# One list of 3388 program steps, put in another order

## Chip, core and metric

One core of a Trainium2 chip runs the whole kernel in one launch. The metric is the device time in microseconds (us); lower is better. Five instruction streams run side by side and meet at semaphores: TensorE (PE, with its weight loads PEld), VectorE (DVE), ScalarE (ACT), GpSimd (POOL) and the sync engine (SP), which issues nearly all DMAs.

## The reference, cut

```python
def reference(**kwargs):
    attn_out = _attn_ref(**attn_kwargs)   # 4 batches x 8 heads, 512 local + 32 global queries, head size 64
    x = attn_out.transpose(0, 2, 1, 3).reshape(B * S, H * D)          # 2176 x 512
    x = _moe_ref(x=x, **moe_kwargs)       # max(x@w1, x@w2, x@w3) @ w_out, width 768
    return _moe2_ref(x=x, **moe2_kwargs)  # (sigmoid(x@w_gate) * (x@w_val)) @ w_out2, width 1536
```

The local queries see a window of 32 positions to each side and the 32 global keys; the global queries see everything. All of it is float32.

## The kernel before

The kernel computes in stages that overlap. Attention is cut into 32 units t = 0 to 31 (4 batches x 2 halves of the sequence x 4 pairs of heads). Four units make a chunk c = 0 to 7 of 256 or 288 tokens, and each chunk then goes through the first feed-forward layer (the maximum of three products, and its output product). After the last chunk come the gate and value products over all tokens (line L1048) and the output product (L1235); these two use seven products in place of eight for a 2x2 block product. Float32 precision is kept by splitting an operand in a high and a low part and adding three products (`mm3`, L321 to L323).

Every piece of work is a generator whose parts are put into a list `ev`: 3388 steps, each a few instructions, with a planned time (L1303 onwards). The order in which the steps are run, and so the order of each engine's instruction stream, isn't the planned one, though: it is the list `ORDER` (L22) of 3388 step numbers, written out. Each engine works through its own steps strictly in that order. If a step waits, all later steps of that engine wait with it.

The steps that are named below; the last number of a step is its part:

- lg(c, what): whole-chunk loads of q, k, v for the first two chunks (`at_load_group`, L422). lqk(t): 8 loads of q and k of a unit (L517, L518). lv(t): 4 loads of v into the tile vr (`load_v_rows`, L497 to L503), of which there is one buffer only. g(b, 0): loads of the global queries and values (L384, L389); g(b, 1): their transpose on DVE (L392).
- pqk(t, .): transposes of q and k. sc(t, 0): the score products (L627). sm(t, .): softmax on ACT and DVE, whose part 11 is the last subtraction into pc on DVE (L715) and whose part 12 is a transposing DMA pt<-pc on SP (L718). smg is the same for the global queries, with the DMA in part 7 (L761).
- pv(t, .): v is split in three 16-bit parts: part 0 casts on ACT (L599), 1 subtracts on POOL (L601), 2 casts on DVE (L603), 3 subtracts on POOL (L605) and is the last to read vr. lv(t) must therefore wait for pv(t-1, 3), and pv(t, 0) for the landing of lv(t).
- av(t, 0), avg(t, .), scg(t, 0): the products with v, and those of the global queries. l1(c, f, w, 0): 12 products of the first layer (L892, L906 and L900 read the result); l2(c, m, .): 18 products of its output. wa(i, 0): load of a weight block (L302, L305).

`at_load_group`, `load_v_rows` and the other generators are not touched by the change.

Of the kernel before, what the change touches and what calls it, by code (L numbers as in the profile page):

```python
# [22 lines left out]
    57, 153, 186, 154, 155, 304, 56, 59, 187, 120, 0, 62, 58, 63, 64, 67, 68, 69, 74, 75, 70, 121, 161, 71, 162, 76,  # L23
    77, 78, 1861, 1862, 79, 5, 6, 163, 1863, 1864, 156, 188, 7, 8, 122, 1854, 1855, 95, 96, 166, 167, 168, 1856, 80,
    1865, 1857, 97, 1833, 123, 81, 82, 1858, 1866, 1826, 194, 100, 101, 189, 102, 103, 195, 98, 87, 88, 72, 9, 10, 11,
    104, 12, 1827, 1828, 337, 13, 173, 14, 83, 128, 15, 129, 99, 107, 289, 108, 105, 109, 60, 110, 1834, 169, 208, 170,
    130, 131, 111, 112, 1829, 209, 231, 1835, 106, 174, 89, 133, 1830, 124, 157, 232, 233, 113, 16, 90, 114, 91, 115,
    1831, 116, 190, 175, 176, 134, 135, 136, 137, 198, 1840, 199, 125, 200, 140, 141, 142, 143, 177, 1836, 178, 117,
    144, 145, 126, 305, 92, 93, 1847, 1841, 223, 279, 179, 61, 1875, 180, 224, 225, 226, 1903, 84, 203, 181, 1848, 182,
    1849, 204, 205, 146, 206, 147, 148, 207, 280, 85, 86, 236, 234, 149, 150, 256, 1850, 257, 1851, 1842, 210, 211,  # L30
    1837, 1843, 1844, 241, 237, 242, 264, 212, 213, 171, 138, 191, 214, 215, 192, 158, 1867, 1868, 201, 238, 159, 1322,
    1324, 281, 1852, 1904, 1876, 1859, 290, 227, 239, 265, 1323, 1877, 216, 1905, 1869, 1917, 1326, 17, 243, 1860,
    1870, 1325, 1878, 1879, 1906, 244, 240, 1832, 312, 132, 245, 246, 313, 314, 284, 1882, 1889, 1890, 164, 217, 1896,
    1327, 139, 1880, 218, 1316, 1314, 285, 286, 247, 248, 1891, 1871, 1872, 1315, 1907, 287, 288, 1892, 196, 1893,
    1853, 249, 1938, 315, 1883, 1884, 1885, 165, 250, 1897, 1898, 1899, 266, 1900, 1901, 317, 1902, 1317, 1910, 1886,
    1338, 1339, 318, 360, 362, 1340, 1341, 73, 1939, 183, 319, 1342, 202, 251, 1940, 338, 1845, 118, 1911, 219, 252,
    1931, 320, 321, 1918, 151, 267, 1343, 1952, 1846, 1919, 1932, 1933, 228, 229, 1941, 363, 324, 291, 1912, 1881, 253,
    292, 1934, 293, 325, 1330, 1332, 1942, 1, 396, 1344, 326, 1318, 294, 1331, 316, 268, 258, 1920, 160, 230, 1935,
    364, 1319, 368, 1328, 259, 260, 261, 1924, 282, 283, 1838, 1921, 235, 1980, 269, 197, 295, 1953, 270, 296, 1945,
    398, 271, 262, 263, 1334, 1908, 1913, 399, 1914, 2, 297, 1839, 1954, 1887, 1894, 1333, 298, 1925, 1348, 1926, 339,  # L40
    94, 369, 1981, 1335, 306, 1909, 299, 300, 1955, 1956, 1946, 1947, 1959, 1346, 370, 1354, 371, 152, 327, 328, 329,
    372, 1948, 1355, 1336, 1949, 18, 19, 1895, 404, 220, 1329, 1960, 322, 1961, 1927, 1928, 1888, 323, 273, 1962, 274,
    1982, 275, 1347, 1349, 1963, 330, 1356, 1357, 20, 331, 307, 308, 21, 272, 22, 400, 23, 332, 1358, 1973, 333, 1350,
    1966, 24, 25, 345, 1974, 1975, 309, 1976, 1929, 1977, 1967, 1983, 26, 340, 341, 342, 373, 1984, 1968, 1969, 184,
    185, 254, 334, 1970, 375, 1930, 1987, 376, 405, 1985, 127, 1988, 1337, 221, 310, 406, 343, 1351, 1989, 27, 1366,
    28, 1359, 1374, 407, 1957, 1990, 1991, 365, 1367, 1375, 411, 468, 335, 361, 470, 377, 378, 412, 471, 379, 346, 413,
    408, 432, 347, 1958, 3, 4, 380, 1362, 366, 434, 388, 1986, 472, 1376, 1363, 1370, 276, 1371, 344, 414, 348, 349,
    415, 381, 416, 350, 435, 436, 401, 193, 1368, 1369, 437, 382, 438, 1873, 445, 383, 367, 351, 1377, 352, 440, 389,
    390, 1992, 311, 1874, 1964, 354, 353, 409, 391, 1965, 355, 356, 357, 384, 1364, 397, 417, 1372, 385, 1993, 1922,
    1923, 336, 473, 591, 1378, 358, 424, 1320, 1386, 425, 386, 418, 441, 504, 301, 419, 420, 1387, 1388, 1389, 277,  # L50
    1379, 426, 1978, 255, 1979, 1915, 476, 1390, 1380, 1382, 442, 427, 1391, 359, 278, 29, 447, 428, 448, 1936, 1937,
    1373, 443, 444, 593, 1381, 449, 450, 1383, 387, 1402, 506, 507, 421, 1384, 1916, 451, 1392, 1396, 422, 1971, 477,
    483, 433, 478, 484, 1394, 1393, 512, 479, 640, 480, 1403, 460, 594, 474, 1385, 452, 446, 392, 1352, 393, 1972, 423,
    1395, 1397, 1950, 453, 508, 454, 455, 456, 457, 458, 481, 461, 462, 485, 1406, 1398, 1399, 1404, 1943, 1418, 540,
    1400, 1405, 1407, 595, 1353, 513, 596, 514, 542, 459, 1410, 486, 1360, 515, 482, 516, 519, 410, 429, 520, 463, 464,
    465, 521, 522, 487, 488, 489, 466, 543, 544, 641, 490, 509, 510, 523, 1944, 1401, 469, 599, 1419, 172, 491, 524,
    492, 525, 493, 494, 1951, 1422, 1408, 1409, 496, 497, 600, 627, 601, 1365, 498, 1411, 30, 606, 1412, 499, 607,
    1413, 1414, 1415, 430, 222, 602, 431, 603, 1416, 1417, 1420, 1421, 608, 500, 609, 394, 610, 1423, 611, 526, 467,
    597, 1424, 527, 528, 374, 495, 1361, 612, 613, 614, 505, 1425, 1321, 1438, 545, 1426, 529, 1427, 530, 615, 531,
    546, 547, 1428, 1439, 532, 548, 1440, 549, 517, 553, 550, 551, 555, 533, 678, 534, 535, 616, 395, 501, 502, 552,  # L60
    302, 1430, 503, 1466, 402, 629, 556, 557, 558, 559, 560, 561, 630, 631, 562, 1431, 1442, 563, 564, 565, 1441, 536,
    635, 1443, 541, 604, 617, 1432, 537, 566, 567, 636, 637, 554, 638, 639, 1468, 576, 577, 1467, 1469, 578, 579, 568,
    569, 570, 571, 572, 642, 643, 1470, 1429, 1471, 1444, 1445, 605, 1434, 680, 65, 580, 581, 714, 582, 592, 1446,
    1450, 1447, 1435, 1472, 1436, 663, 1448, 1454, 1452, 644, 403, 645, 573, 681, 583, 585, 664, 646, 586, 1449, 1451,
    1453, 786, 686, 647, 1455, 619, 475, 648, 620, 621, 622, 687, 1458, 688, 716, 1456, 649, 650, 1457, 31, 32, 1473,
    689, 651, 1462, 690, 652, 1460, 1459, 717, 33, 34, 538, 628, 1461, 1433, 587, 574, 575, 1463, 655, 1464, 653, 656,
    632, 693, 1474, 727, 35, 1475, 36, 1478, 1437, 1476, 588, 589, 37, 38, 39, 1477, 1479, 1486, 1482, 1465, 1484, 40,
    657, 41, 722, 42, 750, 584, 691, 694, 1483, 1485, 1487, 654, 1480, 658, 598, 1481, 1490, 679, 695, 1502, 665, 723,
    729, 666, 724, 730, 752, 1488, 667, 668, 1489, 1491, 725, 590, 731, 1503, 696, 1504, 618, 511, 669, 670, 697, 1498,
    698, 623, 753, 754, 1492, 1493, 726, 1499, 732, 733, 624, 788, 789, 699, 718, 700, 701, 706, 707, 659, 660, 661,  # L70
    734, 822, 1500, 1501, 858, 662, 692, 682, 702, 703, 704, 625, 708, 709, 672, 673, 674, 675, 676, 539, 1494, 677,
    735, 736, 737, 1495, 758, 626, 738, 739, 794, 795, 796, 740, 1506, 824, 715, 922, 825, 683, 1507, 759, 633, 1530,
    760, 761, 1531, 742, 743, 1508, 1510, 1509, 1496, 1511, 909, 1538, 1512, 765, 766, 767, 1513, 744, 762, 797, 768,
    826, 769, 1532, 1533, 719, 1534, 770, 798, 1497, 745, 1535, 1536, 710, 634, 1516, 741, 771, 772, 773, 774, 775,
    1514, 119, 705, 1537, 711, 763, 776, 66, 860, 751, 778, 830, 831, 777, 1515, 832, 1539, 1518, 779, 801, 833, 802,
    780, 1542, 1517, 1519, 803, 1540, 781, 782, 684, 804, 805, 837, 806, 861, 827, 807, 834, 808, 1526, 809, 866, 783,
    871, 671, 835, 810, 811, 712, 713, 799, 1520, 1521, 787, 814, 815, 812, 1541, 1543, 43, 1522, 911, 836, 816, 746,
    894, 895, 813, 1524, 1544, 1523, 1525, 1527, 1545, 1528, 912, 913, 1546, 867, 1547, 873, 868, 1345, 874, 869, 875,
    1548, 1549, 817, 1505, 818, 823, 850, 1550, 1529, 755, 1551, 945, 996, 1552, 1553, 851, 1554, 784, 785, 870, 876,
# [1407 lines left out]
```

## Time and profile before

| what | us |
|---|---|
| median of 3 runs (lowest, highest) | 803.16 (800.95, 805.37) |
| the profiled execution's own time | 803.19 |
| its span, first to last instruction | 801.5 |
| TensorE busy in the span | 785.0 (98%) |
| TensorE weight loads busy | 753.7 (94%) |
| VectorE, ScalarE, GpSimd busy | 567.8, 471.6, 141.7 |

The profile is read by asking, for TensorE, in which stretches it is idle and what ended each idle time, and then by following what the releasing engine had itself waited for. A line of a timeline gives start, length, engine, line and tiles; a square bracket at its end tells how long the engine was idle just before and who ended that. "SPq" is the sync engine issuing DMAs.

### The profile page before, as it was taken

What the parts mean: (1) busy time and instruction counts of PE and PEld (TensorE: products, weight loads), DVE (VectorE), ACT (ScalarE), POOL (GpSimd) and SP (SyncE); (2) the same over time, 40 slices, a digit from 0 to 9 for tenths busy, and PEclk for the clock granted to TensorE, in tenths of its full rate; (3) what the DMA queues carried; (4) which work ended last, traced back from release to release, by engine and by line L of the source; (5) the groups of instructions that cost most, each with busy time, mean ns of one, the idle gap of its engine ahead of it and who ended that gap; (6) DMA issues with size and microseconds to landing.
All of it is one profiled execution on the core that took longest, in us unless ns stands there. A gap on an engine that the chain in (4) does not pass through costs nothing.

```text
span 801.5 us, 18202 instructions
## 1 busy us (share of the span) xinstructions
PE 785.0 (98%) x6950; PEld 753.7 (94%) x6950; DVE 567.8 (71%) x1249; ACT 471.6 (59%) x1131; POOL 141.7 (18%) x149
## 2 busy tenths in 40 slices
PE   6999999999999999999999999999999999999998
PEld 5888899989899989899999999999999999999998
DVE  4768788667766676774586866777565669977673
ACT  6998867455565564463467665665645466443441
POOL 3125574242323423132110000000000000000000
PEclk9999999999999999999999999999999999999999
DMA  8978464545536564345145464857142578542521
GB/s 238 294 183 222 86 123 87 107 97 103 115 73 122 101 112 89 67 99 159 38 153 186 115 226 159 289 167 242 69 143 105 162 240 312 189 142 86 172 66 53
DMA packets 208887, 116.08 MB, mean 145 GB/s; under 512 B 152864, under 2 KB 191264, under 8 KB 208800
## 3 DMA queue, kind: packets, MB, share of 16 engines
q1 hardware_dynamic: 208512, 114.80, 52.6%
q8 instruction: 54, 0.88, 0.5%
q14 instruction: 33, 0.27, 0.1%
q10 hardware_dynamic: 288, 0.13, 0.1%
HBM read 74.91 MB, written 28.57 MB: 129 GB/s over the span
## 4 chain that ended last, share of the span: by engine, by line
PE 80%; SPq 7%; ACT 5%; DMA 3%; DVE 2%; issue 1%; POOL 1%; ACTq 0%; DVEq 0%; POOLq 0%
PE pa L1048 18%; PE pe L1048 9%; PE pa L1235 9%; PE ps L321 7%; PE ps L323 6%; PE ps L322 6%; PE pb L1048 4%; PE pe L1235 4%; PE ps L892 4%; PE sp L627 3%; PE pb L1235 2%; DMA vr<-in_v_g_dram 2%; SPq L518 2%; SPq L517 1%; PE ps L928 1%
## 5 line engine op out<-in xcount | busy, mean ns | idle before, releaser
L1048 PE MATMUL pa<-m,m 128*128 128x384 f32 (+1 forms) x864 | 154.4, 326 | 0.0
L321 PE MATMUL ps<-xt,m 128*128 128x288 f32 (+1 forms) x504 | 148.1, 294 | 3.9 <-DVE h L906 2.3
L323 PE MATMUL ps<-xt,m 128*128 128x288 f32 (+1 forms) x504 | 146.4, 290 | 0.0
L322 PE MATMUL ps<-xt,m 128*128 128x288 f32 (+1 forms) x504 | 145.3, 288 | 0.8 <-DVE stg L732 0.8
L1048 PEld LDWEIGHTS pa<-m,m 128*128 128x128 f32 x864 | 144.1, 188 | 0.1
L321 PEld LDWEIGHTS ps<-xt,m 128*128 128x128 f32 x504 | 94.7, 188 | 8.6 <-DVE h L906 3.0
L322 PEld LDWEIGHTS ps<-xt,m 128*128 128x128 f32 x504 | 94.7, 188 | 1.0 <-DVE stg L732 1.0
L323 PEld LDWEIGHTS ps<-xt,m 128*128 128x128 f32 x504 | 94.8, 188 | 0.0
L1054 ACT COPY sn<-pa 128x384 f32<-128x384 f32 (+1 forms) x108 | 49.3, 461 | 74.1 <-PE pa L1048 71.3
L1048 PE MATMUL pe<-m,m 128*128 128x384 f32 (+1 forms) x432 | 81.7, 327 | 0.2 <-DVE sgt L1067 0.2
L1048 PEld LDWEIGHTS pe<-m,m 128*128 128x128 f32 x432 | 72.6, 188 | 0.6 <-DVE sgt L1067 0.6
L1235 PE MATMUL pa<-m,m 128*128 128x256 f32 x576 | 72.2, 283 | 0.0
L1235 PEld LDWEIGHTS pa<-m,m 128*128 128x128 f32 x576 | 70.5, 192 | 0.1
L669 ACT ACTIVATE sm<-sm,st 128x224 f32<-128x224 f32 x128 | 60.8, 480 | 16.0 <-DVE st L633 15.6
L906 DVE TENSOR_TENSOR h<-ps,h 128x288 f32<-128x288 f32 (+1 forms) x90 | 39.1, 436 | 32.0 <-PE ps L323 22.3
L715 DVE TENSOR_TENSOR pc<-sm,pc 64x512 f16<-64x512 f32 (+1 forms) x72 | 51.5, 718 | 4.4 <-ACT pc L712 3.4
L271 POOL TENSOR_TENSOR h<-h,h 128x288 fp32r<-128x288 f32 (+1 forms) x42 | 36.0, 862 | 91.8 <-ACT h L911 90.6
L633 DVE CUSTOM_DVE_ANT_0 sm<-sp,mask 128x224 f32<-128x224 f32 x128 | 44.8, 382 | 8.7 <-PE sp L627 6.9
L1178 DVE TENSOR_TENSOR m<-m,m 128x768 fp32r<-128x768 f32 x44 | 40.7, 954 | 13.5 <-ACT m L1173 13.0
L321 PE MATMUL ps<-h,m 128*128 128x288 f32 (+1 forms) x168 | 49.2, 293 | 0.0
L322 PE MATMUL ps<-h,m 128*128 128x288 f32 (+1 forms) x168 | 48.6, 289 | 0.6 <-POOL h L271 0.5
L323 PE MATMUL ps<-h,m 128*128 128x288 f32 (+1 forms) x168 | 48.9, 291 | 0.0
(193 smaller groups left out, 1573.7 us busy)
## 6 DMA issues: line engine op xcount, KB each, us to landing
m<-in_moe_w_dram SPq DMA_DIRECT2D x18, 512.0 KB, 5.8
gd<-sgt SPq DMA_DIRECT2D x48, 192.0 KB, 2.7
m<-gd SPq DMA_DIRECT2D x6, 1536.0 KB, 7.2
m<-in_moe_w_val_dram SPq DMA_DIRECT2D x6, 1024.0 KB, 5.6
wr<-in_moe_w_out_dram SPq DMA_DIRECT2D x6, 1024.0 KB, 6.0
m<-in_moe_w_gate_dram SPq DMA_DIRECT2D x5, 1024.0 KB, 5.6
vr<-in_v_l_dram SPq DMA_DIRECT2D x48, 96.0 KB, 2.5
x2d<-x2s SPq DMA_DIRECT2D x32, 128.0 KB, 2.0
```

The costliest lines, as they stand in the source:

```text
L271: nc.gpsimd.tensor_tensor(out=out, in0=a, in1=f32(b), op=ALU.subtract)
L321: nc.tensor.matmul(ps, lhsT=wh, rhs=xh, start=first, stop=False)
L322: nc.tensor.matmul(ps, lhsT=wh, rhs=xl, start=False, stop=False)
L323: nc.tensor.matmul(ps, lhsT=wl, rhs=xh, start=False, stop=last)
L633: nc.vector.tensor_tensor_reduce(out=sm[:, hh, j], in0=sp[hh][:, j, 0:224], in1=mask[:, half + j, :], scale=-SC, scalar=3.0e38, op0=ALU.ad ...
L669: nc.scalar.activation(sm4[:, i], sm4[:, i], AF.Exp, bias=st[:, 0, i:i + 1], scale=-1.0, accum_out=st[:, 2, i:i + 1])
L715: nc.vector.tensor_tensor(out=l_, in0=s_, in1=h_, op=ALU.subtract)
L906: nc.vector.tensor_tensor(out=a, in0=ps[:, 0:n], in1=a, op=ALU.max)
L1048: nc.tensor.matmul(ps, lhsT=w[l][:, a, i], rhs=x[m][:, i], start=(k in (1, 2, 5) and i + l + m == 0), stop=(k in (2, 3, 4) and i == 1 and ...
L1054: nc.scalar.copy(t[:, 0:n], pend[u]["a"][:, 0:n])
L1178: tt(out=lo, in0=src[op], in1=f32(hi), op=ALU.subtract)
L1235: nc.tensor.matmul(ps, lhsT=g[l][:, f], rhs=wo_op(b, f, m), start=(k in (1, 2, 5) and f + l + m == 0), stop=(k in (2, 3, 4) and f == 5 and ...
```

## The change

`ORDER` is replaced by another permutation of the same 3388 numbers. Nothing else differs: the same steps, instructions, tiles and transfers. According to its author the new list is the outcome of a search on a model of the schedule in which the sync engine is held longer by each transfer. 423 of the 650 TensorE steps stand at another place among TensorE's steps, most of them by a few places; each unit and chunk is begun within a few us of TensorE work of where it was.

The diff is 346 lines of numbers. Of it, the lines with the steps that are spoken of:

```diff
 ORDER = [
-    57, 153, 186, 154, 155, 304, 56, 59, 187, 120, 0, 62, 58, 63, 64, 67, 68, 69, 74, 75, 70, 121, 161, 71, 162, 76,
...
-    1865, 1857, 97, 1833, 123, 81, 82, 1858, 1866, 1826, 194, 100, 101, 189, 102, 103, 195, 98, 87, 88, 72, 9, 10, 11,
...
-    1453, 786, 686, 647, 1455, 619, 475, 648, 620, 621, 622, 687, 1458, 688, 716, 1456, 649, 650, 1457, 31, 32, 1473,
...
-    729, 666, 724, 730, 752, 1488, 667, 668, 1489, 1491, 725, 590, 731, 1503, 696, 1504, 618, 511, 669, 670, 697, 1498,
...
-    1514, 119, 705, 1537, 711, 763, 776, 66, 860, 751, 778, 830, 831, 777, 1515, 832, 1539, 1518, 779, 801, 833, 802,
...
-    1048, 793, 908, 1632, 1624, 1037, 943, 991, 944, 1123, 1027, 1028, 1049, 1050, 1045, 1140, 992, 1081, 993, 994,
...
-    1033, 995, 1060, 1658, 1051, 1176, 1052, 1142, 1660, 55, 1053, 1082, 1054, 1659, 1055, 1124, 1056, 1057, 1058,
...
+    87, 88, 89, 0, 57, 56, 58, 62, 59, 186, 187, 63, 64, 67, 90, 91, 68, 69, 70, 256, 74, 75, 76, 71, 77, 161, 162,
...
+    1830, 209, 195, 190, 1857, 1858, 72, 105, 106, 128, 129, 130, 337, 1831, 1832, 194, 231, 99, 1833, 1834, 1835, 120,
...
+    585, 631, 786, 1472, 1451, 1453, 1455, 1456, 586, 402, 686, 687, 1473, 31, 621, 622, 632, 1458, 1460, 1459, 693,
+    475, 716, 32, 33, 34, 1462, 652, 653, 1461, 1463, 717, 1457, 35, 628, 36, 37, 1474, 1437, 38, 1464, 1475, 1465,
...
+    725, 668, 1502, 1503, 1504, 695, 1490, 1491, 669, 750, 727, 752, 726, 679, 706, 1492, 696, 403, 1361, 729, 670,
...
+    1026, 989, 943, 944, 1027, 1630, 1631, 1028, 1629, 1040, 1632, 980, 1140, 1022, 1621, 1076, 865, 1041, 1121, 990,
...
+    1079, 1178, 1634, 1635, 1046, 1650, 1660, 1659, 1661, 1060, 1061, 1062, 1662, 1663, 1664, 1063, 1636, 1064, 1637,
...
 ]
```

Numbers and steps: 57, 59, 58 = lg(0, q0), lg(0, q1), lg(0, k1); 195, 194 = lg(1, q), lg(1, k); 1833 = wa(1, 0); 31, 32 = g(2, 0), g(2, 1); 704, 705, 711 = sm(16, 11), sm(16, 12), av(16, 0); 669, 670, 672 = smg(15, 6), smg(15, 7), avg(15, 0); 1027, 1033, 1060 = pv(24, 3), lv(25), pv(25, 0).

The stretch from pv(24, 3) to pv(25, 0), with TensorE's and SP's steps alone:

```text
before: pv(24,3)  scg(25,0)  lqk(28)  scg(26,0)  lv(25)  pv(25,0)
after:  pv(24,3)  l2(4,3,0)  l2(4,3,1)  l2(4,2,3)  sc(25,0)  lqk(28)  l2(4,0,3)  sc(26,0)  avg(23,0)  avg(23,1)
        scg(25,0)  lv(25)  lqk(29)  sm(25,12)  scg(26,0)  sm(24,12)  l1(5,3,0,0)  l1(5,0,0,0)  l1(5,2,0,0)
        l1(5,3,1,0)  pv(25,0)
```

The stretch from g(2, 0) to g(2, 1), with TensorE's steps alone:

```text
before: g(2,0)  g(2,1)
after:  g(2,0)  l1(2,2,0,0)  l1(2,2,1,0)  g(2,1)
```

Loads at the beginning, on SP's list: before lg(0,q0), lg(0,q1), lg(0,k1), wa(5,0), g(0,0), wa(4,0), wa(1,0), wa(0,0), lg(1,k), lg(1,q); after lg(0,q0), lg(0,k1), lg(0,q1), wa(5,0), wa(4,0), g(0,0), wa(0,0), lg(1,q), lg(1,k), wa(1,0).

## Rows read from the trace of the kernel before

**Rows 1.** The page: busy time of each engine; the chain that ended last

```profile
PE 785.0 (98%) x6950; PEld 753.7 (94%) x6950; DVE 567.8 (71%) x1249; ACT 471.6 (59%) x1131; POOL 141.7 (18%) x149
...
PE 80%; SPq 7%; ACT 5%; DMA 3%; DVE 2%; issue 1%; POOL 1%; ACTq 0%; DVEq 0%; POOLq 0%
```

**Rows 2.** Busy time by stretches of 20 us: stretch, engines with instruction counts, clock, DMA

```profile
0.00:20.00 20.00, 13.11 (x118) 10.09 (x120) 9.02 (x36) 13.13 (x42) 7.69 (x27) 1.00 0.87 238
...
160.00:180.00 20.00, 18.57 (x174) 17.44 (x168) 12.74 (x41) 11.31 (x34) 9.91 (x11) 1.00 0.48 96
...
200.00:220.00 20.00, 18.88 (x219) 17.34 (x218) 15.97 (x46) 10.61 (x33) 7.73 (x9) 1.00 0.57 113
...
380.00:400.00 20.00, 20.00 (x152) 19.83 (x152) 11.86 (x16) 8.86 (x16) 3.92 (x3) 1.00 0.14 50
...
500.00:520.00 20.00, 20.00 (x124) 20.00 (x122) 14.78 (x32) 13.48 (x23) 0.00 (x0) 1.00 0.84 280
```

**Rows 3.** Waits of TensorE, whole span: us in total, times, longest

```profile
PE tq L541 <- POOL mask L354: 3.2, 1, 3.2
PE ps L321 <- DVE h L906: 2.3, 3, 1.4
PE sp L627 <- ACT kw L565: 2.3, 3, 0.9
PE tq L541 <- DMA m<-in_q_l_dram: 1.4, 1, 1.4
PE ps L321 <- ACT h L900: 1.2, 2, 0.7
PE ps L322 <- DVE stg L732: 0.8, 1, 0.8
PE ot L788 <- DMA pt<-pc: 0.7, 1, 0.7
PE ps L322 <- POOL h L271: 0.5, 1, 0.5
```

**Rows 4.** Waits of ACT and of DVE for loads, 20 to 400 us

```profile
ACT vb L599 <- DMA vr<-in_v_g_dram: 18.3, 10, 3.1
...
DVE qgt L392 <- DMA qgr<-in_q_g_dram: 4.8, 2, 2.9
```

**Rows 5.** SP's issues of two lines: duration ns min/median/max, first and last start

```profile
L518 SPq DMA_DIRECT2D kr<-in_k_l_dram x96: 311/449/2011, 43.2 to 320.8; - x96
...
L718 SPq DMA_TRANSPOSE pt<-pc x24: 1273/1438/2452, 105.0 to 360.3; - x24
```

**Rows 6.** DMA issues of the page's kind: KB each, median us to landing

```profile
vr<-in_v_g_dram SPq DMA_DIRECT2D x24, 16.0 KB, 2.0
pt<-pc SPq DMA_TRANSPOSE x24, 3.8
```

**Rows 7.** Timeline around the longest wait of TensorE past the start

```profile
162.26 1.88 SPq L384 DMA_DIRECT2D qgr<-in_q_g_dram  x4
...
165.44 0.32 DVE L392 STREAM_TRANSPOSE qgt<-qgr 128x128 f32<-128x128 f32 x1 [2.93 <-DMA qgr<-in_q_g_dram]
...
168.72 0.38 PE L321 MATMUL ps<-xt,m 128*128 128x256 f32 x1 [1.43 <-DVE h L906]
```

**Rows 8.** Timeline from pv(24, 3) to pv(25, 0)

```profile
283.09 1.28 POOL L605 TENSOR_TENSOR vb<-vr,vb 128x512 bf16<-128x512 f32 x1 [1.42 <-DVE vb L603]
...
290.73 0.62 ACT L599 CAST vb<-vr 128x512 bf16<-128x512 f32 x1 [3.06 <-DMA vr<-in_v_g_dram]
...
293.27 0.40 PE L321 MATMUL ps<-xt,m 128*128 128x288 f32 x1 [0.70 <-ACT h L900]
```

**Rows 9.** Timeline of the first 20 us: lg(1, q) and pqk(5, 0)

```profile
13.22 2.57 SPq L431 DMA_DIRECT2D m<-in_q_l_dram  x2
...
19.46 0.66 PE L541 MATMUL tq<-ident,m 128*64 128x128 f32 x8 [1.45 <-DMA m<-in_q_l_dram]
```

**Rows 10.** Waits of SP, whole span

```profile
SPq L718 <- PE ps L323: 10.8, 12, 1.6
```

324 rows, old and new, of the table ORDER are left out of this document.

## Prediction

> **What bounds the kernel now.** I read the busy times first, then the stretches, then TensorE's waits, then the waits of the engines that released it. TensorE is busy 785.0 of 801.5 us and 80% of the chain that ended last is TensorE's [rows 1], so nothing but TensorE's idle time, 801.5 - 785.0 = 16.5 us, can be won by an order that leaves every instruction as it is. The stretches say where it lies [rows 2]: 6.9 us in the first 20, then one or two us in single stretches of the attention part (1.4 in 160 to 180, 1.1 in 200 to 220), and none in 500 to 520, which stands for the whole second half. So the change is decided in the first 360 us. 3.2 us of it is the wait for the first instruction, and about as much comes after the last product; neither list changes that. Some 10 us are left.
>
> TensorE's waits name them [rows 3]: 2.3 us for DVE's h (1.4 of it one wait), 1.4 for a load of q, 1.2 for ACT's h, 0.7 for a transposed pt, 0.5 for POOL's h, 0.8 for stg, and 2.3 for kw at the start. Behind most of them stands SP. The wait of 1.4: DVE stood 2.93 us for qgr, whose four loads SP began to issue at 162.26, and the step that TensorE needed came only after that [rows 7]. The ACT waits: ACT stands 18.3 us in 10 of 24 units before the cast of vr, DVE 4.8 us before qgt [rows 4], and what is queued behind (the copies of h, the softmax) is late; after one of 3.06 us TensorE waited 0.70 [rows 8].
>
> SP is the reason, since it is nearly full. A load holds it 0.449 us, a transposing DMA 1.438 [rows 5]. A unit has 8 + 4 loads and one transpose: 12 x 0.449 + 1.438 = 6.8 us, and the 24 units follow each other every (360.3 - 105.0) / 23 = 11.1 us [rows 5], so units alone take 61% of SP, and the weight loads and stores come on top.
>
> At this point a rule speaks against the change. The Trainium skill (DMA: Bandwidth & Descriptors, "Issuing engines are not separate DMA queues") says that the sequencer's time to start a DMA is usually small beside the DMA itself; then where a load stands on SP's list would hardly matter and the time would stay at 803.2. The trace doesn't bear it out for these loads: 0.449 us of issue against 2.0 to landing, and 61% of SP.
>
> **The change, part by part.** It adds and removes no instruction. I compared the two lists by the TensorE work that stands between a step and the one that needs it; TensorE work is close to time here, since TensorE is 98% busy. A product of 288 columns is 0.132 us (20 us / 152 [rows 2]), so an l1 step of 12 is 1.6 us and an l2 step of 18 is 2.4. The rest is sized likewise from its matmuls' count and pitch: sc 0.9, scg 0.6, avg 0.4 and 0.6.
>
> *The single buffer vr.* From the last read of vr, pv(t-1, 3), to its next use, pv(t, 0), POOL's 1.28 [rows 8], four issues (4 x 0.449) and a landing of 2.0 [rows 6] must fit: 5.1 us. Before, the list gives pv(25, 0) two scg steps, 1.2 us; the true distance was 290.73 - 283.09 = 7.6 us, as lqk(28)'s eight issues stood in between [rows 8]. The new list gives 2.2 (l2 in 256 columns) + 1.8 + 1.0 + 1.2 + 6.4 = 12.6 us. The same count for t = 9 to 31, in us:
>
> before: 2.4 5.7 3.4 8.0 9.8 13.9 4.3 7.4 8.3 4.1 4.4 0.0 13.7 6.6 4.3 11.3 1.2 5.9 4.1 2.2 3.7 4.2 11.5
> after: 3.2 7.3 5.9 7.2 11.6 8.2 7.2 6.7 9.0 9.8 1.6 3.2 5.3 7.0 3.9 8.1 12.6 8.0 6.4 10.3 12.4 3.7 1.4
>
> Under 5.1 are 12 before and 6 after; what is missing sums to 23 us before and 14 after. ACT's waits should fall by the same 40%, from 18.3 to about 11 [rows 4]. TensorE's share of them is at most 1.2 + (2.3 - 1.4) + 0.5 = 2.6 us [rows 3]; 40% is 1.1 us won. Bounds: 2.6, if the six that are left hit where TensorE has other work; 0, if they hit harder (t = 19 and 31 are shorter than before).
>
> *g(2) and g(3).* The load and its use stood together; now two l1 steps, 2.9 us, stand between, and for g(3) as much. DVE's waits were 2.93 [rows 7] and 4.8 - 2.93 = 1.9 [rows 4]. The 1.4 us of TensorE go [rows 7]; bounds 0 to 1.6.
>
> *The transpose for av(16).* sm(16, 12) stood right before av(16, 0); now 22.6 us of TensorE work stand between. The 0.7 us [rows 3] go.
>
> *The first 20 us.* pqk(5, 0) waited 1.45 us for lg(1, q) [rows 9]. The new list issues it ahead of lg(1, k) and wa(1, 0), five issues earlier, so it should land in time: 1.4 won, bounds 0 to 1.4. Against it, lg(0, q1) now goes behind the two issues of lg(0, k1): 2 x 0.449 = 0.9 us later for pqk(3, 0), which may wait 0 to 0.9; TensorE then waits for kw anyway (2.3 in three waits [rows 3]), so I take 0.4.
>
> *What is new and tight.* sc(9), sc(15) and sc(28) stand right behind the DVE transposes that they need, with no TensorE step between. Before, only sc(10) and the first units stand so; sc(10) is in no row of the waits, the first units cost up to 0.9 each [rows 3]. Three times 0 to 0.9; nearest is sc(10), so 0.3 each, 0.9 in all. The second half of the list has the same kind of sequence as before (each product 0.9 us or more behind the copy that frees its bank, the end in the same order), and TensorE is never idle there [rows 2]: nothing, and if DVE's cover there (14.8 of 20 us) failed at a place, some tenths.
>
> Sum: -1.1 - 1.4 - 0.7 - 1.4 + 0.4 + 0.9 = -3.3 us. Against the profiled execution's 803.19, which lies on the median of the runs, 803.16, this gives 799.9 us.
>
> **Rivals.** *All of the order's stalls go.* If the new list leaves none of the 2.6, nor stg's 0.8, and sc costs nothing: -2.6 - 1.4 - 0.7 - 1.4 - 0.8 = -6.9, 796.3 us. For: the waits share one cause. Against: six vr distances are still too short.
>
> *The gain is given back.* Six short distances of vr, of which 19, 20 and 31 are 2 to 4 us short, hit TensorE as hard as those of before, and each sc that stands close costs 0.9: -1.4 - 0.7 - 1.4 + 0.9 + 2.7 = +0.1, so 803.3, no change. The rule on SP's issue time above ends here too.
>
> *Slower: transposes stuck behind loads on SP.* Where a transpose is listed after loads that it doesn't need, av waits for them. From DVE's last step to the product the new list gives smg(15) 3.9 us with 12 loads ahead, sm(10) 4.8 with 8, sm(29) 4.5 with 5, sm(18) 7.5 with 12. Needed are 3.8 for the DMA [rows 6] plus 0.449 a load: 9.2, 7.4, 6.0, 9.2. Missing: 5.3 + 2.6 + 1.5 + 1.7 = 11.1 us straight on TensorE: 799.9 + 11.1 = 811.0. It decides if SP has no head start when it reaches these loads; with 2 us at each place 3.9 are left, which is about the time of before. Against it: before, SP stood at 12 transposes waiting for something older than their data, 10.8 us in all [rows 10], so it was mostly early, and the new list spreads its loads more evenly.
>
> *A far larger gain.* Weight loads are busy 753.7 us, 31 less than the products [rows 1]; if that is room, 803.2 - 47.8 + 6 at the ends = 761 at most. The Trainium skill (Perfetto Trace Analysis, "Identifying the Most-Contended Engine") calls matmul busy time a poor measure and wants the weight loads' share; by it there are 47.8 us of room. The rows speak against it as a gain from order: where TensorE has nothing but l1 and l2, weight loads take 19.83 of 20 us, and in the mixed stretch 160 to 180 17.44 with 18.57 of products [rows 2], so most of the gap goes with the small products of attention, which stay.
>
> **How the numbers follow.** My forecast, part of the waits going, spreads from 797.5 to 801.5: 0.48. All go: 0.20 (of which 0.01 for the far larger gain). Given back: 0.19. Slower: 0.13. About 0.5% (4 us, so under 799.1 or over 807.2) is what a measurement of this kernel tells from no change. Faster takes the rival of 0.20 and nearly half of the forecast: 0.42. Slower by that much takes most of the transposes' rival: 0.11. The same: 0.47. The range reaches from 795.0, under the full gain by what the sizes leave open, to 806.0, over the case of no gain by one stuck transpose half paid; 0.1 is left out on each side.
>
> **What would show it.** Right: TensorE idle 12 to 14 us; no wait of DVE for qgr before 170 us; ACT's waits for vr near 11 us; no wait of TensorE for q near 19 us. Wrong: TensorE waiting for DMA pt<-pc by several us (the slower rival), sc waiting for kt or kw by more than 1 us in all past the start, or idle time after 400 us, where I expect none.

## The result, and the profile after

| | before | after |
|---|---|---|
| median, us (lowest, highest; runs) | 803.72 (800.95, 805.37; 4) | 794.81 (794.25, 797.92; 4) |
| ratio, 95% interval | | 0.9902 [0.9882, 0.9922] |
| profiled execution, its span | 803.19, 801.5 | 797.92, 796.2 |
| TensorE busy, idle in the span | 785.0, 16.5 | 784.5, 11.7 |

The new list is faster by 1.0%, some 8 us; 799.9 was forecast, and the result lies 0.2 us under the range (795.0 to 806.0). That it falls outside by so little is chance: a second set of times of the same program (run after_again below) has the median 795.15. What missed is the size, 3.3 us forecast against about 8. The profiled execution happened to be the longest of its four. A second profile, in after_again, took 795.39, with 9.7 us idle in a span of 793.7.

The page of the new kernel, the row that answers to [rows 1]:

```profile
PE 784.5 (99%) x6950; PEld 753.7 (95%) x6950; DVE 567.5 (71%) x1249; ACT 469.3 (59%) x1131; POOL 144.3 (18%) x149
```

Busy time by stretches, new kernel, answering to [rows 2], with two stretches more:

```profile
0.00:20.00 20.00, 14.58 (x125) 10.74 (x125) 9.44 (x37) 13.02 (x43) 6.36 (x26) 1.00 0.85 243
...
160.00:180.00 20.00, 19.41 (x231) 18.32 (x224) 12.98 (x41) 10.10 (x30) 10.30 (x11) 1.00 0.64 101
200.00:220.00 20.00, 19.84 (x226) 18.18 (x226) 14.46 (x44) 11.05 (x31) 8.17 (x8) 1.00 0.53 103
...
280.00:300.00 20.00, 20.00 (x253) 19.00 (x249) 11.90 (x41) 12.86 (x48) 4.31 (x4) 1.00 0.57 112
...
320.00:340.00 20.00, 20.00 (x234) 18.93 (x231) 16.39 (x48) 12.01 (x40) 7.21 (x7) 1.00 0.50 99
```

The same two stretches of the kernel before:

```profile
280.00:300.00 20.00, 18.57 (x235) 16.83 (x232) 15.91 (x52) 13.91 (x48) 5.84 (x5) 1.00 0.65 118
...
320.00:340.00 20.00, 18.73 (x217) 16.95 (x217) 14.67 (x44) 9.80 (x28) 3.89 (x4) 1.00 0.38 67
```

From 280 to 300 and from 320 to 340 us TensorE's busy time was 18.57 and 18.73 of 20 and is now full. At 200 to 220 its idle time fell from 1.12 to 0.16, at 160 to 180 from 1.43 to 0.59.

Waits of TensorE, new kernel (us in total, times, longest), answering to [rows 3]:

```profile
PE tq L541 <- DMA m<-in_q_l_dram: 3.0, 1, 3.0
PE sp L627 <- ACT kw L565: 2.1, 4, 0.7
PE ps L321 <- ACT x2s L935: 0.8, 1, 0.8
PE ps L321 <- DVE h L906: 0.8, 2, 0.6
PE tk L541 <- DVE qw L561: 0.6, 1, 0.6
PE tp L691 <- DVE sm L683: 0.5, 1, 0.5
```

The waits for ACT's h, stg, pt and POOL's h are gone, and DVE's h fell from 2.3 to 0.8. In the second profile the 0.8 for x2s is missing too and DVE's h is 0.2: there the whole rest of the list behind the first 30 us has one wait over 0.15 us, of 0.20, where the list before had ten, of 5.99 in all. But ACT and DVE still wait for loads about as long as before (20 to 400 us, answering to [rows 4]):

```profile
ACT vb L599 <- DMA vr<-in_v_g_dram: 20.2, 13, 2.8
...
DVE qgt L392 <- DMA qgr<-in_q_g_dram: 4.5, 3, 3.4
```

ACT waits 20.2 us for vr against 18.3 (16.0 in the second profile). What changed is where. In units 25, 28, 29 and 30 ACT waited 3.06, 2.55, 1.80 and 1.19 us, 8.6 in all; in both profiles of the new list these four are zero, and in the first one units 14, 16, 20 and 21, which didn't wait or waited less before, wait 1.9 to 2.8 us. Of these TensorE feels at most that of unit 21 (0.8 for x2s at 240.5, right behind it).

Timeline of the new kernel from pv(24, 3) to pv(25, 0), answering to [rows 8]:

```profile
281.46 1.17 POOL L605 TENSOR_TENSOR vb<-vr,vb 128x512 bf16<-128x512 f32 x1 [1.81 <-DVE vb L603]
...
285.15 0.97 SPq L497 DMA_DIRECT2D vr<-in_v_l_dram  x2
...
292.26 0.64 ACT L599 CAST vb<-vr 128x512 bf16<-128x512 f32 x1
```

Between the starts of the last read of vr and of its next use lie 10.8 us, where 7.6 lay, and the cast waits for nothing (no bracket). At the start, answering to [rows 9]:

```profile
19.31 0.66 PE L541 MATMUL tk<-ident,m 128*64 128x128 f32 x8 [0.62 <-DVE qw L561]
```

The wait of 1.45 for q is gone; 0.62 for qw stands in its place.

### The profile page after: what moved, and what is told of

It reads as the page before. It is cut to its first block, busy times and chain, and to the rows that moved or that the text cites. A ratio compares the mean times of both kernels' runs of the same rounds, so it can differ in the third digit from the quotient of the medians.

```text
span 796.2 us, 18206 instructions
## 1 busy us (share of the span) xinstructions
PE 784.5 (99%) x6950; PEld 753.7 (95%) x6950; DVE 567.5 (71%) x1249; ACT 469.3 (59%) x1131; POOL 144.3 (18%) x149
## 4 chain that ended last, share of the span: by engine, by line
PE 83%; SPq 6%; ACT 4%; DMA 3%; DVE 2%; issue 1%; POOL 0%; ACTq 0%; DVEq 0%; POOLq 0%
PE pa L1048 18%; PE pe L1048 9%; PE pa L1235 9%; PE ps L321 8%; PE ps L323 8%; PE ps L322 8%; PE pb L1048 4%; PE pe L1235 4%; PE ps L892 2%; PE sp L627 2%; PE pb L1235 2%; PE ot L788 1%; DMA m<-in_moe_w_out_dram 1%; DMA vr<-in_v_g_dram 1%; SPq L517 1%; ACT sm L669 1%
## 5 line engine op out<-in xcount | busy, mean ns | idle before, releaser
L669 ACT ACTIVATE sm<-sm,st 128x224 f32<-128x224 f32 x128 | 60.9, 480 | 12.8 <-DVE st L633 12.6
L906 DVE TENSOR_TENSOR h<-ps,h 128x288 f32<-128x288 f32 (+1 forms) x90 | 39.2, 436 | 35.9 <-PE ps L323 26.6
L1178 DVE TENSOR_TENSOR m<-m,m 128x768 fp32r<-128x768 f32 x44 | 41.1, 954 | 24.5 <-ACT m L1173 24.1
L1173 ACT CAST m<-m 128x768 fp32r<-128x768 f32 x44 | 35.3, 836 | 35.5 <-PE pa L1235 12.6
L712 ACT CAST pc<-sm 64x512 f16<-64x512 f32 (+1 forms) x72 | 39.3, 546 | 19.9 <-DVE sm L683 15.1
L321 PE MATMUL ps<-h,m 128*128 128x288 f32 (+1 forms) x168 | 49.3, 294 | 0.0
```

The source lines that it names most:

```text
L321: nc.tensor.matmul(ps, lhsT=wh, rhs=xh, start=first, stop=False)
L669: nc.scalar.activation(sm4[:, i], sm4[:, i], AF.Exp, bias=st[:, 0, i:i + 1], scale=-1.0, accum_out=st[:, 2, i:i + 1])
L712: nc.scalar.copy(d, s_)
L906: nc.vector.tensor_tensor(out=a, in0=ps[:, 0:n], in1=a, op=ALU.max)
L1178: tt(out=lo, in0=src[op], in1=f32(hi), op=ALU.subtract)
```

## The experiments

Each was timed against the old kernel on the same chip. To see where a list loses time I use a curve beside the waits: the start of each TensorE product less the summed pitch of all TensorE work that the list puts ahead of it. A rise between two places is time lost there (us, by TensorE work done). The pitch of a product is worked out from the traces, and the rises hold more than waits: before's curve rises by 14.9 between 40 and 360, where its waits sum to 5.7. So it is the difference between two curves that is read:

| work done | 40 | 140 | 160 | 200 | 260 | 280 | 320 | 360 | 770 |
|---|---|---|---|---|---|---|---|---|---|
| before | 9.1 | 11.7 | 13.6 | 16.1 | 17.7 | 20.3 | 22.9 | 24.0 | 24.9 |
| after_again | 9.2 | 12.4 | 12.5 | 14.1 | 15.3 | 15.7 | 16.4 | 16.7 | 17.1 |
| pv_late | 9.3 | 12.1 | 14.1 | 16.6 | 17.4 | 19.3 | 22.7 | 23.4 | 24.1 |
| clusters | 8.9 | 11.6 | 12.3 | 15.3 | 16.2 | 16.9 | 18.4 | 19.1 | 19.8 |
| kr_pool | 9.1 | 14.5 | 14.6 | 16.8 | 22.6 | 23.3 | 24.1 | 24.7 | 25.4 |
| kr_once | 9.0 | 11.9 | 11.9 | 12.6 | 13.7 | 14.2 | 15.3 | 15.5 | 15.9 |

By this curve the new list wins nothing in the first 40 us, is 0.7 behind at 140, loses 1.7 where the old one lost 4.4 between 140 and 200, and 1.4 against 6.3 between 260 and 360.

### Which stretch of the list carries it

Three kernels: the new one again; *head_new*, with the new list's steps up to 250 us of TensorE work and all others in the old order; *tail_new*, the other way round. The lists are cut at that point, no other line differs.

> The changed kernel unaltered, for a second trace and a second set of times. All theories: 794 to 798 us, TensorE idle 11 to 12 us in the trace, and no wait of TensorE over 0.3 us between 260 and 360 us. If its trace shows other waits than the first one, single waits of some tenths are accidents of the run and only the stretches count.

> The new list up to 250 us of TensorE work, the steps that are left in the order of the old list. Theory V (the gain comes from units 25 to 30, whose cast of vr stands farther from the last read of vr): 802 to 804 us, no gain, and TensorE's waits between 285 and 350 us come back with about 3 us. Rival H (the gain is spread over the attention part, as the bunched loads of SP are): 799, about half of the gain.

> The old list up to 250 us of TensorE work, the steps that are left in the order of the new list. Theory V: 796 to 799 us, at least 5 us under before, with the waits at 169, 207 and 209 us as before and none between 285 and 350. Rival H: 799 to 800, the other half.

Measured: after_again 795.15, ratio 0.9903 [0.9886, 0.9919]; head_new 800.78, 0.9975 [0.9961, 0.9989]; tail_new 798.57, 0.9949 [0.9929, 0.9969]; before 802.77. So the gain is spread: 2.0 us in the head and 4.2 in the tail, 6.2 of 7.6 in all; the 1.4 that are missing lie within the intervals. Theory V, all of it in units 25 to 30, doesn't hold, though most of it lies there. In head_new TensorE waits at 291.7, 294.3, 328.3, 331.2 and 345.3 us (1.23, 0.73, 0.67, 0.76, 0.63), at the five places where before waits (0.70, 0.73, 0.51, 0.76, 0.33); in tail_new there is none between 285 and 350, while 1.54 at 168.7, 0.58 for pt at 206.7 and 0.96 at 209.7 stand.

### Is it the single buffer vr?

```diff
-        vr = at.tile([P, 2, 4, D], F32, tag="vr", name="vr")
+        vr = mem(1024 * 24 + 512 * (t % 4), (2, 4, D)) if t >= 16 else at.tile([P, 2, 4, D], F32, tag="vr", name="vr")
```

From unit 16 on vr rotates through four buffers; *vr2_before* has the old list, *vr2_after* the new one.

> The old list, but from unit 16 on vr has four buffers in memory that is free by then, so lv(t) no longer waits for the last read of the unit before. Theory V (the distance to the last read of vr is what made ACT and then TensorE wait): ACT's waits for vr fall from 18.3 to under 6 us, TensorE's waits between 285 and 350 us mostly go, 799 to 801 us. Rival S (SP is simply too full, the buffer is not what holds the loads): ACT's waits stay above 12 us and the time stays at 803.

> The new list, with vr in four buffers from unit 16 on, in place of one. ACT's waits for vr, 16 to 20 us in the new list, should fall below 12. Theory V in its strict form (in the new list none of these waits reaches TensorE): the time of the new list, 794.8 to 795.3, within 0.5. Rival (they still cost TensorE many waits of under 0.15 us each): 1 to 2 us faster than the new list, 793 to 794, with TensorE's idle time down from 9.5 to 8.5 or less.

Measured: vr2_before 800.38, 0.9971 [0.9955, 0.9988]; ACT's waits for vr are 12.7 us (9.5 in 6 in the new buffers, 3.2 in 3 before them), and TensorE's between 285 and 350 us fall from 3.0 to 0.7. vr2_after 795.07 against 803.3, 0.9903 [0.9885, 0.9922]: the same as the new list. So in the old list the buffer is worth some 2.4 us of the 8, which is between the two theories: the time is V's, ACT's waits are S's. Four buffers don't end the waits: lv(25) still goes out behind lqk(28) on SP. In the new list ACT's waits for vr are still 14.6 us with four buffers, and TensorE has no wait over 0.15 us past the first 30: those waits cost nothing.

### Repairing the old list at single places

```diff
 pv_late
-... scg(26,0) lv(25) [pv(25,0)] l1(5,3,0,0) ... l1(5,0,0,1) pv(25,1)
+... scg(26,0) lv(25) l1(5,3,0,0) ... l1(5,0,0,1) [pv(25,0)] pv(25,1)
 (likewise pv(28,0) to pv(28,1); pv(29,0), pv(29,1) to pv(29,2); pv(30,0) to pv(30,1))
 g_late
-g(2,0) [g(2,1)] ... l1(2,2,2,0) ... l1(2,2,1,0) l1(2,2,0,1) pqk(17,1) g(2,2)
+g(2,0) ... l1(2,2,2,0) ... l1(2,2,1,0) l1(2,2,0,1) pqk(17,1) [g(2,1)] g(2,2)
-sm(16,11) av(14,1) ... sm(17,12) [sm(16,12)] av(16,0)
+sm(16,11) [sm(16,12)] av(14,1) ... sm(17,12) av(16,0)
 (likewise g(3,1) to g(3,2))
```

*few_moves* has both. The move of g(3,1) passes no other step of DVE, and that of pv(29,1) no other step of POOL, so these two leave the instruction order of their engine as it was.

> The old list with five of its 3388 steps moved: pv(25,0), pv(28,0), pv(30,0), each to just before the part 1 that follows it, and pv(29,0) and pv(29,1) to just before pv(29,2); so ACT asks for vr 6.4, 2.1, 7.7 and 2.9 us of TensorE work later in units 25, 28, 29 and 30, and nothing on SP moves. Theory V (late gain: ACT stands before a vr that has not landed, and the copies of h behind it are late): TensorE's waits of 0.70 and 0.73 near 293 to 296 and of 0.51, 0.76 and 0.33 near 330 to 347 go, 3.0 us, so about 799.8. Theory S (the loads are late on SP itself, whatever ACT does): the waits move to av of these units (PE waiting for vb) and the time stays at 802 to 803. Theory H (the gain comes from the order of everything): within 0.8 us of the old list.

> The old list with three steps moved: g(2,1) and g(3,1), DVE's transposes of the global queries, to just before g(2,2) and g(3,2) (two l1 steps and one l1 step of TensorE later), and sm(16,12), the transposing DMA, 19.5 us of TensorE work earlier, behind sm(16,11). By the prediction's terms the 1.43 us of TensorE near 169 and the 0.65 for pt near 207 go, 2.1 us: about 800.7, and DVE's wait of 2.9 us for qgr near 165 falls below 1. Rival: DVE is late there anyway, or the transpose issued early holds SP and makes lqk or lv late: 802 to 803 with new waits of TensorE between 160 and 215.

> The eight moves of the two runs before in one list. If the change's gain is carried by a dozen steps that stood before data that had not come, the two gains add: 3.0 + 2.1 = 5.1 us, about 797.7, two thirds of what the whole new list gives. If the gain comes from the order of everything (theory H), under 2 us: above 800.8.

Measured, before 803.3: pv_late 802.49, 0.9994 [0.9982, 1.0006]; g_late 805.2, 1.0025 [1.0008, 1.0041]; few_moves 803.55, 0.9997 [0.9982, 1.0013]. None wins, and g_late is even slower by 0.25%, though the waits that they were made for shrink. In pv_late ACT's waits for vr fell by half (waits of ACT, 20 to 400 us), and the wait of unit 25 is gone:

```profile
ACT vb L600 <- DMA vr<-in_v_g_dram: 9.7, 6, 2.7
```

Yet at the same place TensorE still stands (timeline of pv_late; its lines are one further down, so L907 is the L906 of before):

```profile
293.96 0.45 DVE L578 STREAM_TRANSPOSE qt<-qr 128x256 f32<-128x256 f32 x1 [1.49 <-DMA qr<-in_q_l_dram]
294.33 0.98 DVE L907 TENSOR_TENSOR h<-ps,h 128x288 f32<-128x288 f32 x2
...
294.81 0.40 PE L322 MATMUL ps<-xt,m 128*128 128x288 f32 x1 [0.87 <-DVE h L907]
```

Now DVE waits 1.49 us for qr of unit 29, whose loads stand behind lv(25) on SP, and the h that TensorE needs is queued behind that. Before, DVE came to this transpose only at 295.02, held back by ACT's stop for vr (it waited 1.46 us for ACT's pc near 292), and qr was there. Near 330 the reason is a plainer one: pv(28,0) was moved by 2.1 us only, ACT still waits 2.33 us for vr of unit 28 (2.55 before), and TensorE's two waits there stay (0.58 and 0.77). g_late shows at its first place what pv_late shows near 294:

```profile
165.83 0.31 DVE L393 STREAM_TRANSPOSE qgt<-qgr 128x128 f32<-128x128 f32 x1 [0.44 <-DMA qgr<-in_q_g_dram]
...
169.59 0.62 ACT L600 CAST vb<-vr 128x512 bf16<-128x512 f32 x1 [2.00 <-DMA vr<-in_v_g_dram]
...
171.29 0.39 PE L322 MATMUL ps<-xt,m 128*128 128x256 f32 x1 [1.19 <-ACT h L901]
```

DVE's wait for qgr fell from 2.93 [rows 7] to 0.44, TensorE's wait at 169 became one of 1.19 at 171, behind a load of vr. A new one of 1.92 came at 204.7, and the trace shows the early transpose behind it: on SP it now goes out right ahead of lv(17), whose last load starts at 197.91 where it started at 195.71, ACT's wait for that vr grows from 2.56 to 5.04 us, and DVE, which makes the next part of v from it, comes late to the h that TensorE needs (timeline of g_late):

```profile
199.99 0.62 ACT L600 CAST vb<-vr 128x512 bf16<-128x512 f32 x1 [5.04 <-DMA vr<-in_v_g_dram]
...
204.71 0.40 PE L322 MATMUL ps<-xt,m 128*128 128x288 f32 x1 [1.92 <-DVE h L907]
```

That is the rival of g_late's expectation (802 to 803 there, 805.2 measured). So theory V falls as I had put it: near 294 ACT's stop before vr was one of two late loads, and curing one alone doesn't decide.

### Is it SP's order, or the order of the others?

From 100 us of TensorE work on, *sp_new100* takes SP's steps in the order of the new list and everything else in the old order; *sp_old100* the reverse. Some 65 of SP's steps stand at another place on SP's list; the lists of the other four engines are untouched.

> From 100 us of TensorE work on, SP works through its steps in the order of the new list; TensorE, ACT, DVE and POOL keep the whole old order. Theory S (the gain comes from where the loads and transposes stand on SP's list): about three quarters of the gain behind 100 us, so 797 to 798. Theory C (it comes from how the steps of TensorE, ACT, DVE and POOL are interleaved, the loads only follow): 802 to 804, or worse, as SP's order then fits the others' less.

> The new list, but from 100 us of TensorE work on SP works through its steps in the order of the old list. Theory S: the gain is lost, 801 to 803. Theory C: 795 to 796.5, most of the gain stays. If both orders must fit each other, both of the mixed kernels are slower than the lists that they are made of: above 803 here and with the old compute order.

Measured, before 803.19: sp_new100 815.45, 1.0148 [1.0121, 1.0175]; sp_old100 806.52, 1.0037 [1.0024, 1.0051]. Neither order holds the gain; each needs the other. The largest wait of TensorE in sp_new100:

```profile
PE ot L789 <- DMA pt<-pc: 4.5, 1, 4.5
```

This is my slower rival, a transpose stuck on SP ahead of av, in a kernel where the two orders don't fit. What holds SP there is not the time of the issues that the rival counted, though: sm(18,12) stands behind lqk(23), and SP stands 6.4 us at a load of k until DVE frees its buffer (waits of SP in sp_new100):

```profile
SPq L519 <- DVE kt L590: 6.4, 1, 6.4
```

In sp_old100 (waits of DVE, then of TensorE) it is a load of q:

```profile
DVE qt L579 <- DMA qr<-in_q_l_dram: 14.3, 3, 10.2
```

```profile
PE ps L323 <- DVE h L908: 7.0, 2, 6.3
```

### Is SP too full?

```diff
 kr_pool
-                dma(out=kr[p0:p0 + 32], in_=k_l[...])
+                nc.gpsimd.dma_start(out=kr[p0:p0 + 32], in_=k_l[...])
 kr_once
-        kr = at.tile([P, 9, 32], F32, tag="kr", name="kr", bufs=2)
+        if t == 16:
+            u["krx"] = mem(1024 * 24, (9, 32))
+        kr = u["krx"] if t >= 16 else at.tile([P, 9, 32], F32, tag="kr", name="kr", bufs=2)
-                dma(out=kr[p0:p0 + 32], in_=k_l[...])
+                t > 16 or dma(out=kr[p0:p0 + 32], in_=k_l[...])
```

> The old list, with the four loads of k of each unit (L518) issued by POOL in place of SP, so that SP has 4 x 0.449 = 1.8 us less to issue in the 11.1 us of a unit. Theory S in its second form (SP is too full, whatever the order): the loads of vr and qr come earlier, TensorE's waits at 169, 207 and 293 to 347 shrink by more than half, 798 to 799. Theory C: these waits stay, 802 to 803.5; POOL's issues may add to the waits for POOL's h.

> The old list; from unit 17 on the four loads of k of each unit (L518) are left out and kt is made from one k that unit 16 loaded, so the scores of these units are of other data, and SP issues 4 x 0.449 = 1.8 us less in each 11.1 us. Nothing is put on another engine. SP too full: the loads of vr and qr come in time, ACT's waits for vr fall from 18.3 below 9 and TensorE's waits past 200 us (0.7 + 0.5 + 0.2 + 0.7 + 0.7 + 0.5 + 0.8 + 0.3 = 4.4) fall under 1.5, so 799.5 to 800.5. If the compute engines' own order is what holds TensorE, these waits stay and the time is 802 to 803.5.

Measured: kr_pool 805.23 against 803.19, 1.0022 [1.0009, 1.0034]; kr_once 795.49 against 802.62, 0.9909 [0.9893, 0.9925]. kr_once moves no step and wins as much as the new list, more than expected. TensorE's waits are of three kinds, and none lies between 21 and 420 us; the second fence has ACT's for vr (20 to 400 us):

```profile
PE tq L543 <- DMA m<-in_q_l_dram: 3.9, 2, 3.1
PE sp L629 <- ACT kw L567: 2.1, 3, 0.7
PE pe L1050 <- DVE sgt L1069: 0.2, 1, 0.2
```

```profile
ACT vb L601 <- DMA vr<-in_v_g_dram: 4.5, 5, 1.5
```

Leaving loads out also takes their bytes from the DMA engines, so the time of kr_once alone doesn't say whether it is the issues or the transfers. The landings do: from issue to landing the loads of vr take as long as before (the largest of them, DMA issues of before, then of kr_once; KB each, median us to landing):

```profile
vr<-in_v_l_dram SPq DMA_DIRECT2D x48, 96.0 KB, 2.5
```

```profile
vr<-in_v_l_dram SPq DMA_DIRECT2D x48, 96.0 KB, 2.4
```

What changed is how full SP is: added up from the timelines of its issues, they take 37.1 of the 40 us from 160 to 200 and 50.4 of the 60 from 260 to 320 before, and 27.8 and 40.1 in kr_once. kr_pool keeps the bytes and moves the issues: late, from 280 to 360, its curve loses 1.4 us where before lost 3.7, and ACT's waits for vr are 8.7 against 18.3. Both point to SP's issues, and not to the transfers; kr_pool does so less cleanly, as TensorE comes to that stretch some 3 us late, which gives SP time. What kr_pool wins there it loses elsewhere, as POOL issues the loads of k behind its own waits (waits of DVE in kr_pool):

```profile
DVE kt L582 <- DMA kr<-in_k_l_dram: 10.1, 4, 4.2
```

The Trainium skill (DMA: Bandwidth & Descriptors, "Issuing engines are not separate DMA queues") says that issuing from more engines saves only the sequencer's time, usually small beside the DMA. The measurements speak against "small" for this kernel: four issues of 0.449 us fewer per unit, and the late stretches flow.

### All the late steps of a place at once

*clusters* is the old list with 14 steps moved, the ones of pv_late and g(2,1) among them, but at each place with the next one that would be late:

```text
 g(2,1) to g(2,2); pv(15,0) one and pv(15,1) three l1 steps later
 sm(16,12) ahead of lqk(22); pv(18,0), pv(18,1) behind sc(20,0) and an l1 step
 pv(25,0) to pv(25,1) and pqk(29,0) to pqk(29,1)
 pv(28,0), pv(28,1) behind l2(5,3,1), pv(28,2) to pv(28,3); pv(29,0), pv(29,1), pv(30,0) as in pv_late
```

> The old list with 14 steps moved, so that in each of the three clusters of waits every step that waits for a load comes later, not one of them alone: g(2,1) and pv(15,0), pv(15,1) near 165; sm(16,12) ahead of lqk(22), and pv(18,0), pv(18,1) near 207; pv(25,0) and pqk(29,0) near 293; pv(28,0) to pv(28,2), pv(29,0), pv(29,1) and pv(30,0) near 330. Stacked waits (behind each late load stands another that is only hidden by it, so one repair moves the wait and all together remove it): TensorE's waits past 160 us fall from 5.5 to under 2.5, so 799 to 800. Whole order (a list moved at a few places always brings new waits of the same size): 802 to 804.

Measured: 798.08 against 802.62, 0.9950 [0.9937, 0.9964], 4.5 us won, more than half of the new list's gain with 14 of 3388 steps. TensorE's waits for h past the start (DVE's, ACT's):

```profile
PE ps L322 <- DVE h L907: 1.0, 3, 0.4
PE ps L322 <- ACT h L901: 0.4, 1, 0.4
```

Past 160 us TensorE waits 2.2 us in all, against 6.0. few_moves, with eight steps at the same places and one more, won nothing. Two pairs can be told apart. Near 294, pqk(29,0) beside pv(25,0) is what pv_late lacked: in pv_late the curve still rose by 1.9 between 260 and 280, here by 0.7. Near 169, pv(15,0) beside g(2,1) is what g_late lacked: its wait of 1.19 is 0.31 here. Near 207 the transpose now stands behind lv(17), and near 330 pv(28,0) was moved farther; these two are better repairs and no proof of a stack.

### Is the room in front of vr needed in the new list?

```diff
 pv_early
-... scg(26,0) sm(24,12) l1(5,3,0,0) ... l1(5,3,1,1) [pv(25,0)] pv(25,1)
+... scg(26,0) sm(24,12) [pv(25,0)] l1(5,3,0,0) ... l1(5,3,1,1) pv(25,1)
-pv(27,3) lv(28) sm(28,6) l1(5,5,1,0) l1(5,5,0,0) ... l2(5,3,1) smg(29,0) [pv(28,0)]
+pv(27,3) lv(28) sm(28,6) l1(5,5,1,0) [pv(28,0)] l1(5,5,0,0) ... l2(5,3,1) smg(29,0)
-l1(6,0,0,0) l1(6,1,0,0) ... sm(28,12) [lv(29) pv(29,0)] sc(30,3)
+l1(6,0,0,0) [lv(29) pv(29,0)] l1(6,1,0,0) ... sm(28,12) sc(30,3)
```

> The new list with pv(25,0) 6.4 us and pv(28,0) 8.8 us of TensorE work earlier, and lv(29) and pv(29,0) 9.1 us earlier, about where the old list has them against their vr. If room in front of the cast of vr is what the new list wins there, ACT waits for vr 2 to 5 us more and TensorE's waits between 280 and 340 come back in part: 796 to 797.5. If the new list has cover behind these steps anyway: 794.8 to 795.5.

Measured: 805.59 against 802.62, 1.0033 [1.0018, 1.0049]: four steps take back the whole gain and more, some 10 us where 1 to 2.5 were expected. The timeline around 321 us:

```profile
321.50 0.62 ACT L601 CAST vb<-vr 128x512 bf16<-128x512 f32 x1 [5.00 <-DMA vr<-in_v_g_dram]
322.03 0.38 ACT L806 ACTIVATE xt<-ot 128x256 fp32r<-128x256 f32 x1
...
324.71 1.28 PE L790 MATMUL ot<-pt,vb 128*64 128x64 f16 x40 [4.66 <-DVE xt L808]
```

ACT stands 5.00 us before vr(28); behind it are its copy of ot and then DVE's read of the same bank, and TensorE waits 4.66 us for it. A wait of 4.05 for vr(29) costs 2.65 at 340. Unit 25 costs nothing: ACT reaches that cast at 289.4, after vr has come. The direction was right, the size far off; a part of it is the clock (last section). lv(29) moved on SP too, ahead of a transpose, so this run is no test of the casts alone.

## Why the prediction missed

*What bounds the kernel* held in the main: idle time of TensorE in the first 360 us, behind loads that come late because SP is nearly full. kr_once shows it most plainly. So did the answer to the rule on issue time. Not quite right was that an order can win nothing but idle time: TensorE's busy time fell too, by 0.5 and 1.0 us in the two profiles.

*The step that failed is the vr term.* It had two parts, and both failed. The first was that a unit waits where its distance is under 5.1 us, so that 40% less missing distance takes 40% off ACT's waits. They were 20.2 and 16.0 us, not 11, and 10 of the 13 waits of the first profile stand in units with more than 5.1: units 14, 16 and 17 had 8.2, 6.7 and 9.0 us and waited 2.80, 1.86 and 2.39 us all the same (new kernel, units 14 and 17):

```profile
157.13 0.62 ACT L599 CAST vb<-vr 128x512 bf16<-128x512 f32 x1 [2.80 <-DMA vr<-in_v_g_dram]
...
200.06 0.62 ACT L599 CAST vb<-vr 128x512 bf16<-128x512 f32 x1 [2.39 <-DMA vr<-in_v_g_dram]
```

The count leaves out what else SP has to issue before it comes to lv(t); what held it for these units was not traced. The second part was that TensorE gets back the same 40%, of at most 2.6 us. Of these 2.6 us 2.4 went, while ACT's waits stayed. A wait of ACT has no price of its own: in these runs it cost where TensorE soon needed what was queued behind it, and nothing elsewhere. The units to look at were those whose waits stood beside TensorE's, 25 and 28 to 30: there the distances went from 1.2, 2.2, 3.7 and 4.2 to 12.6, 10.3, 12.4 and 3.7, and all four waits were gone. A sum over 23 units hid the first three; unit 30 the distance doesn't explain.

Term by term, against the second profile of the new kernel (span 801.5 to 793.7, 7.8 us, 4.5 more than the sum of 3.3): waits for h of ACT, DVE and POOL, 4.0 before [rows 3], are 0.2, so 3.8 where vr and g were given 2.5; stg 0.8, which the sum put at nothing without a reason and which stood only in a rival; pt 0.7, as forecast; x2s and sgt 0.6, not forecast; the three tight sc cost nothing where 0.9 was set against the gain. That is 5.8 past the first 30 us. At the start idle time fell by 0.9 (6.88 to 5.95 in waits), near the 1.0 forecast, but the curve shows no time won by 40 us of work; this was not resolved. The last 1.0 is the busy time, 785.0 to 784.0. So the 4.5 are, to a tenth, 1.3 of vr (2.4 where 1.1 stood), 0.8, 0.6, 0.9 and 1.0: the vr term is the largest part, and not the whole.

Of the four signs that were named as right, one came: no wait for q near 19 us. TensorE's idle time was 11.7 and 9.7 where 12 to 14 stood, DVE still waited for qgr before 170 us, and ACT's waits for vr weren't near 11. None of the signs of being wrong came.

*g(2) and g(3)*: 1.4 us went in the second profile (0.59 stayed in the first), but not by the step I named. DVE still waited 3.4 us for qgr in the new kernel (2.0 in the second profile), and g_late, which cured that wait, won nothing.

*The rival "all of the order's stalls go"*, 796.3, is what happened past the start; it had 0.20. *Given back* is what the partial repairs did. *Stuck transposes* didn't occur in the new list, and one did in sp_new100. *Weight loads*: their busy time is 753.7 in both kernels (754.5 in the second profile), so there was no gain of that kind.

What stays open: beyond the two pairs near 169 and 294, which waits are bound to which. clusters treats the places together, and the 2.7 us that its curve ends above the new list's (0.9 of them there by 260, 1.5 more by 360) were not traced to steps.

## What to carry to other kernels

When one in-order queue feeds several engines and is nearly full, a wait that a trace shows can hide another: ask of each what would be late next if it went, and change all of a place together. A step that is moved on the full queue delays what it passes. Price a wait by what is queued behind it and how soon TensorE needs that, unit by unit, never by a share of a sum. Before searching for an order, test the queue: leave out a third of its loads and see whether the stalls go, and whether the other loads still take as long to land.

## What the runs showed of the hardware

The stand of TensorE in pv_early cost more than itself. TensorE did nothing from 320 to 324.7 us, and the granted clock (the third number from the right) fell to 0.50, the lower of its two levels (1.2 GHz), and stayed there while the work had begun again:

```profile
316.00:320.00 4.00, 4.00 (x69) 3.26 (x68) 0.56 (x4) 0.50 (x1) 2.68 (x3) 1.00 0.17 39
320.00:324.00 4.00, 0.05 (x2) 0.00 (x0) 1.17 (x4) 2.02 (x5) 0.00 (x0) 0.76 0.44 79
...
326.00:328.00 2.00, 2.00 (x11) 1.66 (x8) 0.97 (x2) 1.93 (x10) 0.20 (x1) 0.50 0.00 0
328.00:330.00 2.00, 2.00 (x14) 2.00 (x14) 1.94 (x5) 0.00 (x0) 0.00 (x0) 0.77 0.00 0
330.00:332.00 2.00, 2.00 (x18) 2.00 (x17) 1.95 (x5) 0.40 (x1) 1.09 (x1) 1.00 0.21 68
```

0.77 in 328 to 330 means that it rose near 328.9 (0.92 us at 0.50, the rest at 1.00). So by estimate 4.2 us of work ran at half speed, 2.1 us lost. With the waits, 4.66 and 2.65, that is 9.4 us: the kernel's curve parts from after_again's by 0.7 at 280 and by 10.1 at 320. The stands of 4.54 us in sp_new100 and of 6.33 in sp_old100 were likewise followed by work at 0.50; the waits of 2.65 in pv_early and of 1.92 in g_late left the clock at 1.00.
